# Mask, pooled scaling and value sums of batches 0 and 1 on other engines, and another order of weight chunks for the first three token tiles

## The chip, the core and the metric

The kernel runs on one core of a Trainium2 chip. A core has five engines that run their own instruction streams side by side and wait for each other by semaphores: TensorE (PE, matmuls, with its weight loads as PEld), VectorE (DVE), ScalarE (ACT), GpSimd (POOL) and SyncE (SP, which issues most DMAs). The metric is the device time of one execution in microseconds. Before the change the median of three runs is 1007.32 us.

## The reference

```python
q_d, k_d, v_d = (a.reshape(B, H, 144, 4, D).mean(axis=3) for a in (q, k, v))   # B, H, S, D = 8, 8, 576, 64
out_up = np.repeat(sm_attn(q_d, k_d, v_d), 4, axis=2)
mask = np.abs(pos[:, None] - pos[None, :]) < 4
scores = np.where(mask, scale * q @ k.T, -1e9)            # scale = 1 / 8
out_local = softmax(scores) @ v
x = (out_up + out_local).transpose(0, 2, 1, 3).reshape(4608, 512)
h = x @ w_in                                              # w_in 512 x 2048
out = (h * np.cos(h)) @ w_out                             # w_out 2048 x 512
```

Each head has two attentions: a pooled one over 144 means of four neighbours, and a local one in which a query sees only the keys within three positions. Their sum is the input of a feed-forward layer with the activation h cos h. The weights come as 64-bit floats.

## The kernel before

**Feed-forward.** The 4608 tokens are cut into 12 tiles of 384, and the 2048 hidden features into 16 chunks of 128. A step is one tile with one chunk: `gemm1` makes h (12 matmuls, since x and the weights are each split into a high and a low part), ScalarE and VectorE make h cos h and split it again (lines 748 to 757), and two steps later `gemm2` multiplies by the chunk of `w_out` into three PSUM banks (9 matmuls, line 775). The list `PASSES` (line 36) says in which order tiles and chunks are taken. Tiles 3 to 11 take all 16 chunks at one stretch. Tiles 0 to 2 take four chunks at a time in turn, tile by tile, because the weights of later chunks are not there yet. At the end of each stretch the banks are evacuated and stored; a later stretch of the same tile adds to what is in DRAM (a DMA from GpSimd, line 800).

**Weights.** Each chunk has two halves of 512 KB, one of `w_in`, one of `w_out`. `w_load` brings a half, `w_split` turns the 64-bit words into a high and a low 32-bit part: one operation on ScalarE, four on VectorE (lines 421, 423, 425, 427), then a copy and a subtraction.

**Attention.** A unit is one batch with a pair of heads; there are 32. Its steps are

- `u_qk`: loads of q and k, and the pooling of both (line 490 on VectorE, or 483 and 485 on GpSimd).
- `u_v`: loads of v, and the sums of four neighbours in two additions (lines 504 and 505, on either engine).
- `u_s`: local scores (`l_mm`, line 546) and pooled scores (`d_mm`, line 555) into two PSUM banks; the mask is added on the way out of PSUM (line 569), then maximum (574), subtraction (399), exponentials on ScalarE (594 and 597 for batches 0 and 1), sums (609), reciprocal (611 and 613), and scaling of both parts by it (615, or 621 on ScalarE for the pooled part of batches 0 and 1).
- `u_t`: transposes of the pooled weights on TensorE (line 648), evacuated by line 465 or 466; the local weights are transposed by VectorE (line 632).
- `u_pv`: products with the values, pooled (line 665) and local (677), and their sum (lines 465 and 696), which is copied into x (lines 711 and 399).

`NEARLY = 2`: batches 0 and 1 are done in a form of their own, ahead of everything else, since tile 0 is made of batch 0 alone and tile 1 of batches 0 and 1. Their units borrow the places of weight chunks that have not come yet. Three PSUM banks serve `u_s`, `u_t` and `u_pv` of batch 1 in turn, so a pair's scores wait until the pair before has given up its banks.

**What sets the order.** All operations go into a plan with an assumed duration, and a list scheduler (`Plan`) decides in which order each engine takes them; operations with `alts` may go to another engine, and it decides that too. When an assumed duration, an engine or the order of the steps changes, the order on all engines changes. While TensorE would be idle early in the program, line 892 has it multiply an identity to no purpose.

## Time and profile before

| | |
|---|---|
| median of three runs | 1007.32 us (1006.21 to 1008.86) |
| the profiled execution | 1007.4 us, of which the profile's span is 1005.6 us |
| TensorE busy | 981.2 us (98% of the span) |
| VectorE busy | 681.7 us (68%) |
| ScalarE busy | 610.2 us (61%) |
| GpSimd busy | 221.3 us (22%) |
| mean granted clock of TensorE | 0.988 |
| `gemm1` matmuls, line 739 | 2304, 338 ns each in the record, overlapping |
| `gemm2` matmuls, line 775 | 1728, 396 ns each in the record, overlapping |

A row of a group reads: line, engine, operation, output and inputs by the program's names, their shapes, count, busy us, mean ns of one, then the idle time of the engine before them and what ended it. A row of the timeline begins with the start and the length in us. A row of the windows begins with the stretch and its length, then each engine's busy time with its number of instructions, the clock of TensorE, the share of the DMA engines and GB/s. Matmuls overlap, so the length of one in the record is longer than its share of the time. Names such as wxi and wxo are weight places that a unit borrows.

### The profile page before, as it was taken

Reading aid. Unit: us, or ns where it says so; the run is one execution under the profiler, and the core shown is the slowest. Engines: PE = TensorE matmul, PEld = TensorE weight load, DVE = VectorE, ACT = ScalarE, POOL = GpSimd, SP = SyncE. Lnnn points to the kernel's source line nnn. Section 1 sums busy time; section 2 is a strip of 40 time slices with the busy share of each in tenths; the row PEclk is TensorE's granted clock in tenths of the full one; section 3 lists DMA queues with packets and bytes.
Section 4 is the critical chain, followed back from the end, with each engine's and each line's share of the span. In section 5 each row is a group of like instructions: output and inputs, shape, how many; then the busy total and the mean of one; then the engine's idle time right before and its main releaser. Section 6 shows DMA issues by size and latency. Waiting matters only on the chain.

```text
span 1005.6 us, 23855 instructions
## 1 busy us (share of the span) xinstructions
PE 981.2 (98%) x9917; PEld 847.3 (84%) x9917; DVE 681.7 (68%) x1362; ACT 610.2 (61%) x1174; POOL 221.3 (22%) x280
## 2 busy tenths in 40 slices
PE   8878999999999999999999999999999999999998
PEld 4546899899887888889888888888888888899997
DVE  7799899986587578464758957655657865433433
ACT  3457588876576656555547746654646665655554
POOL 6775325631153202000002211200001300000000
PEclk9979799999999999999999999999999999999999
DMA  7784643424355322210212312201112320100000
GB/s 224 234 270 149 215 159 64 80 36 68 67 116 132 78 65 70 68 33 28 81 49 71 129 49 58 83 26 36 62 54 73 112 65 4 37 1 1 32 1 32
DMA packets 41051, 80.70 MB, mean 80 GB/s; under 512 B 4976, under 2 KB 16240, under 8 KB 40944
## 3 DMA queue, kind: packets, MB, share of 16 engines
q1 hardware_dynamic: 37056, 72.11, 23.2%
q0 software_dynamic: 3888, 7.08, 5.0%
q8 instruction: 78, 1.28, 0.5%
q14 instruction: 29, 0.24, 0.1%
HBM read 57.93 MB, written 16.52 MB: 74 GB/s over the span
## 4 chain that ended last, share of the span: by engine, by line
PE 87%; DVE 6%; DMA 4%; issue 1%; ACT 1%; SPq 0%; ACTq 0%; DVEq 0%
PE bank L775 38%; PE bank L739 38%; PE bank L539 2%; PE bank L684 2%; PE bank L555 2%; PE bank L665 2%; PE bank L648 1%; DMA q<-qT 1%; DMA wdi<-w_in 1%; PE bank L892 1%; PE bank L677 1%; DMA vl<-vl 1%; DVE su L609 1%; DMA wxi<-qT 0%; DVE wxo L615 0%
## 5 line engine op out<-in xcount | busy, mean ns | idle before, releaser
L775 PE MATMUL bank<-wo,gh 128*128 128x512 f32 x1152 | 363.5, 396 | 0.0
L775 PEld LDWEIGHTS bank<-wo,gh 128*128 128x128 f32 x1152 | 210.0, 188 | 38.0 <-issue 3.1
L775 PE MATMUL bank<-wo,gl 128*128 128x512 f32 x576 | 227.6, 396 | 0.0
L750 ACT ACTIVATE tr<-bank,bmagic 128x384 f32<-128x384 f32 x192 | 110.9, 577 | 113.5 <-PE bank L739 109.7
L754 DVE SCALAR_TENSOR_TENSOR tr<-tr,bank 128x384 f32<-128x384 f32 x192 | 105.0, 547 | 108.0 <-ACT tr L749 107.1
L751 DVE SCALAR_TENSOR_TENSOR tr<-tr,bank 128x384 f32<-128x384 f32 x192 | 105.6, 550 | 84.2 <-ACT tr L750 83.2
L748 ACT ACTIVATE tr<-tr 128x384 f32<-128x384 f32 x192 | 100.7, 524 | 77.0 <-DVE tr L751 76.4
L756 ACT ACTIVATE gh<-tr 128x384 fp32r<-128x384 f32 x163 | 85.3, 523 | 88.3 <-DVE tr L754 86.8
L399 DVE TENSOR_TENSOR gl<-tr,gh 128x384 fp32r<-128x384 f32 x154 | 92.4, 600 | 63.5 <-ACT gh L756 60.5
L775 PEld LDWEIGHTS bank<-wo,gl 128*128 128x128 f32 x576 | 108.0, 187 | 23.5
L739 PE MATMUL bank<-x0h,wi 128*128 128x384 f32 x384 | 107.5, 340 | 0.0
L739 PE MATMUL bank<-x1h,wi 128*128 128x384 f32 x384 | 107.1, 339 | 0.0
L739 PE MATMUL bank<-x2h,wi 128*128 128x384 f32 x384 | 106.8, 338 | 0.0
L739 PE MATMUL bank<-x3h,wi 128*128 128x384 f32 x384 | 106.5, 338 | 0.0
L749 ACT ACTIVATE tr<-tr 128x384 f32<-128x384 f32 x192 | 100.8, 525 | 6.1
L399 POOL TENSOR_TENSOR gl<-tr,gh 128x384 fp32r<-128x384 f32 x38 | 43.0, 1132 | 269.6 <-DVE gh L757 175.8
L739 PEld LDWEIGHTS bank<-x0h,wi 128*128 128x128 f32 x384 | 70.5, 189 | 2.6 <-issue 0.5
L739 PEld LDWEIGHTS bank<-x1h,wi 128*128 128x128 f32 x384 | 70.3, 188 | 2.6 <-issue 0.6
L739 PEld LDWEIGHTS bank<-x2h,wi 128*128 128x128 f32 x384 | 70.2, 188 | 2.3 <-issue 0.4
L739 PEld LDWEIGHTS bank<-x3h,wi 128*128 128x128 f32 x384 | 70.2, 188 | 2.0
L739 PE MATMUL bank<-x0l,wi 128*128 128x384 f32 x192 | 64.6, 337 | 0.0
L739 PE MATMUL bank<-x3l,wi 128*128 128x384 f32 x192 | 64.6, 336 | 0.0
(199 smaller groups left out, 1452.6 us busy)
## 6 DMA issues: line engine op xcount, KB each, us to landing
vl<-vl SPq DMA_DIRECT2D x26, 384.0 KB
out<-ob SPq DMA_DIRECT2D x36, 256.0 KB
wdi<-w_in SPq DMA_DIRECT2D x16, 512.0 KB
wdo<-w_out SPq DMA_DIRECT2D x16, 512.0 KB
q<-qT SPq DMA_DIRECT2D x26, 292.0 KB
k<-kT SPq DMA_DIRECT2D x26, 292.0 KB
vd<-vdn SPq DMA_DIRECT2D x26, 288.0 KB
out<-ob POOLq DMA_DIRECT2D x27, 256.0 KB, 5.2
```

The source lines that it names most:

```text
L399: f = lambda e: lambda: e.tensor_tensor(out=out(), in0=in0(), in1=in1(), op=ALU.subtract)
L539: pe.matmul(banks[h].get()[BS * g:BS * (g + 1), c:c + BS], q.get()[hs, o:o + BS], k.get()[hs, o:o + BS], start=True, stop=True)
L555: pe.matmul(banks[h].get()[:HD, i * SD:(i + 1) * SD], qkd.get()[hs, 0, i * HD:(i + 1) * HD], qkd.get()[hs, 1, :], start=True, stop=True)
L665: pe.matmul(banks[0].get()[64 * h:64 * h + 64, 2 * SD:3 * SD], vd.get()[:, kh, 64 * h:64 * h + 64], ptd.get()[:, h, kh, :], start=(kh == 0 ...
L739: pe.matmul(ph.get()[:, :m], w[:, i, kc, :], x[:, kc, :], start=(n == 0), stop=(n == 3 * KC - 1))
L748: act.activation(tr.get(), tr.get(), AF.Sin, scale=PI)
L749: act.activation(tr.get(), tr.get(), AF.Square)
L750: pl.op("ACT", _act(m, True, 1), lambda: act.activation(tr.get(), h(), AF.Identity, bias=bmagic), r=[ph], w=[tr])
L751: pl.op("DVE", _dve(m), lambda: dve.scalar_tensor_tensor(out=tr.get(), in0=tr.get(), scalar=MAGIC, in1=h(), op0=ALU.subtract, op1=ALU.subt ...
L754: pl.op("DVE", _dve(m), lambda: dve.scalar_tensor_tensor(out=tr.get(), in0=tr.get(), scalar=0.5, in1=h(), op0=ALU.subtract, op1=ALU.mult), ...
L756: pl.op("ACT", _act(m, False), lambda: act.activation(gh.get(), tr.get(), AF.Copy), r=[tr], w=[gh], alts=[("DVE", _dve(m / 2), lambda: dve ...
L775: pe.matmul(o, (gh, gh, gl)[k].get()[:, sl], wo.get()[:, (0, 1, 0)[k]], start=(c == c0 and k == 0), stop=(c == c1 - 1 and k == 2))
```

## The change

It has four parts.

1. *Mask.* For batches 0 and 1, two matmuls of an identity with the mask (now bf16) write the mask into both PSUM banks, and the local scores are accumulated on it. VectorE then takes the maxima and subtracts them straight from PSUM, one half (192 columns) at a time, in place of an addition, a maximum over 384 columns and a subtraction over 384 columns.
2. *Pooled scaling.* For batches 0 and 1 it always goes to ScalarE, as four instructions; it was GpSimd, VectorE or ScalarE as the planner saw fit.
3. *Value sums.* For batches 0 and 1 the sums of four neighbours are not made; the pooled product takes the four rows one after another, 16 accumulated matmuls (32 instructions) in place of 4 (8 instructions).
4. *Order of chunks.* Tiles 0 to 2 take chunks 0 to 3 in turn, then chunks 4 to 7, then chunks 8 to 15 at one stretch, in place of four stretches of four.

```diff
-PASSES = [(t, c, c + NF) for c in range(0, NC, NF) for t in range(3)] + [(t, 0, NC) for t in range(3, NT)]
+PASSES = [(t, c, e) for c, e in ((0, NF), (NF, 2 * NF), (2 * NF, NC)) for t in range(3)] + [(t, 0, NC) for t in range(3, NT)]
...
-    mask = const.tile([P, NSEG + 1, BS], F32, name="mask")
+    mask = const.tile([P, NSEG + 1, BS], BF16, name="mask")
...
         dma(4 * P * 12 * D, lambda: sp.dma_start(vt.get(), vl[b, pr]), w=[vt])
+        if b < NEARLY:
+            st[(b, pr)].update(vd=vd4, vl=vt)
+            return
...
+            if b < NEARLY:
+                for h in range(2):
+                    pe.matmul(banks[h].get()[:, LQ:LQ + NSEG * BS], ident_b, mask[:, h:h + NSEG].rearrange("p s n -> p (s n)"),
+                              start=True, stop=False)
...
-                                  q.get()[hs, o:o + BS], k.get()[hs, o:o + BS], start=True, stop=True)
+                                  q.get()[hs, o:o + BS], k.get()[hs, o:o + BS], start=False, stop=(n % NSEG == NSEG - 1))
         if b < NEARLY:
-            pl.op("PE", 0.95, l_mm, r=[q, k], pw=banks, w=loc)
+            pl.op("PE", 1.3, l_mm, r=[q, k], pw=banks, w=loc)
...
+        if b < NEARLY:
+            for h in range(2):
+                mx = pl.buf(None)
+                using(banks[h], pl.op("DVE", _dve(NSEG * BS), lambda h=h: dve.tensor_reduce(
+                    out=segs(mxl, h), in_=lq(h), axis=AX.X, op=ALU.max), r=[loc[h]], pw=[mxl], w=[mx]))
+                using(banks[h], pl.op("DVE", _dve(NSEG * BS), lambda h=h: dve.tensor_tensor(
+                    out=segs(sml, h), in0=lq(h), in1=segs(mxl, h).unsqueeze(2).broadcast_to([P, NSEG, BS]), op=ALU.subtract),
+                    r=[loc[h], mx], pw=[sml]))
...
-                alts.append(("ACT", 4 * _act(SD, False, 1), scaled))
-            pl.op("POOL", _pool(size), f(pool), r=[su], w=[sm], alts=alts, shares=True)
+                pl.op("ACT", 4 * _act(SD, False, 2), scaled, r=[su], w=[sm])
+            else:
+                pl.op("POOL", _pool(size), f(pool), r=[su], w=[sm], alts=alts, shares=True)
...
+            if b < NEARLY:
+                for i in range(8):
+                    for h in range(2):
+                        pe.matmul(banks[0].get()[64 * h:64 * h + 64, 2 * SD:3 * SD], vd.get()[:, i, 64 * h:64 * h + 64],
+                                  ptd.get()[:, h, i // 4, :], start=(i == 0), stop=(i == 7))
+                return
...
-            pl.op("PE", 0.64, d_mm, r=[vd, ptd], pw=[banks[0]], w=[poo])
+            pl.op("PE", 2.1, d_mm, r=[vd, ptd], pw=[banks[0]], w=[poo])
```

The lines below the edits move down by up to 24: 546 becomes 553 for the scores, 555 becomes 562, 648 becomes 666, 665 becomes 684, 677 becomes 701, 739 becomes 763, 775 becomes 799.

Three places show how the planner's order moves. The first is TensorE where the last pair of batch 1 takes its turn (L648 and L666 are the transposes of the third pair, L546 and L553 the local scores of the last pair, L555 and L562 its pooled scores, L665 and L684 the pooled product of the third pair, L739 a step of tile 0, L775 and L799 `gemm2` of an earlier step). Before:

```order
L648 MATMUL bank<-ident,wxo_197 72x72 x8
L546 MATMUL bank<-wxo_933,wxo_923 32x32 x48
L555 MATMUL bank<-wxi_214 72x144 x4
L665 MATMUL bank<-wxi_200 64x144 x4
L739 MATMUL bank<-x0h,wi_1488 128x384
```

And now:

```order
L666 MATMUL bank<-ident,wxo_199 72x72 x4
L799 MATMUL bank<-wo_1226,gh 128x512 x2
L799 MATMUL bank<-wo_1226,gl 128x512
L666 MATMUL bank<-ident,wxo_199 72x72 x4
L538 LDWEIGHTS ident_b
L538 MATMUL bank<-mask,ident_b 128x192
L538 LDWEIGHTS ident_b
L538 MATMUL bank<-mask,ident_b 128x192
L553 MATMUL bank<-wxo_974,wxo_909 32x32 x48
L562 MATMUL bank<-wxi_205 72x144 x4
L684 MATMUL bank<-wxi_202,wxo_495 64x144 x16
```

The longer pooled product (16 matmuls in the place of 4) stands behind the next pair's scores, as before; the fourth step of tile 0 stood behind it and has moved ahead of the transposes.

The second place is VectorE at the sums of the third pair of batch 1 (L609 and L626 are its sums, L611, L613 and L628, L630 the reciprocal, L615 the pooled scaling, L632 and L650 its local transpose; L421 to L427 and L399 with a name wo are weights, L696 and L720 the addition for the second pair, L751, L754, L775 and L778 belong to steps). Before:

```order
L609 TENSOR_REDUCE su<-wxo_390 128x12
L432 CAST wi_1488<-xxh 128x512
L611 TENSOR_SCALAR su<-su 128x16
L427 SCALAR_TENSOR_TENSOR xxh<-wdo_948,xxh 128x512
L613 RECIPROCAL su<-su 128x16
L696 TENSOR_TENSOR wxi_308<-bank,wxi_276 128x3x96
L615 TENSOR_TENSOR wxo_197<-wxo_197,su 72x576
L696 TENSOR_TENSOR wxi_308<-bank,wxi_276 128x3x96
L632 STREAM_TRANSPOSE wxo_390<-wxo_390 128x384
```

And now:

```order
L626 TENSOR_REDUCE su<-wxo_399 128x12
L399 TENSOR_TENSOR wo_1506<-xxh,wo_1506 128x512
L628 TENSOR_SCALAR su<-su 128x16
L423 TENSOR_SCALAR xxh<-xxh 128x512
L630 RECIPROCAL su<-su 128x16
L425 SCALAR_TENSOR_TENSOR xxh<-wdo_1284,xxh 128x512
L778 SCALAR_TENSOR_TENSOR tr<-tr,bank 128x384
L427 SCALAR_TENSOR_TENSOR xxh<-wdo_1284,xxh 128x512
L650 STREAM_TRANSPOSE wxo_399<-wxo_399 128x384
```

The scaling has left VectorE, and more of the weights' operations stand between the pair's own.

The third place is SyncE, where the last halves of the weights are fetched (wdi and wdo are halves of `w_in` and `w_out`, out is a store of a stretch's result, ptb, q and vd belong to batch 2). Before:

```order
L797 DMA out<-ob 128x512 x3
L410 DMA wdi_2019<-w_in 128x4x256
L410 DMA wdo_2051<-w_out 128x1024
L410 DMA wdi_2063<-w_in 128x4x256
L410 DMA wdo_2095<-w_out 128x1024
L410 DMA wdi_2107<-w_in 128x4x256
L410 DMA wdo_2138<-w_out 128x1024
L410 DMA wdi_2151<-w_in 128x4x256
L797 DMA out<-ob 128x512 x3
L410 DMA wdo_2210<-w_out 128x1024
```

And now:

```order
L410 DMA wdi_2059<-w_in 128x4x256
L821 DMA out<-ob 128x512 x2
L410 DMA wdo_2110<-w_out 128x1024
L821 DMA out<-ob 128x512
L410 DMA wdi_2147<-w_in 128x4x256
L410 DMA wdo_2163<-w_out 128x1024
L410 DMA wdi_2192<-w_in 128x4x256
L410 DMA wdo_2206<-w_out 128x1024
L476 DMA q<-qT 128x584
```

All weights are now fetched ahead of the stores of tiles 1 and 2's first stretch, which stood in part before the last half.

More of the change, by code (lines that the diff above doesn't have):

```diff
@@ L567, in u_s @@
         pl.op("POOL", 0.15, lambda: pool.memset(su.get(), 1.0), w=[su])
-        for h in range(2):
-            using(banks[h], pl.op("DVE", _dve(NSEG * BS), lambda h=h: dve.tensor_tensor(
-                out=sml.get()[:, NSEG * h:NSEG * (h + 1)], in0=banks[h].get()[:, LQ:LQ + NSEG * BS].rearrange("p (s n) -> p s n", n=BS),
-                in1=mask[:, h:h + NSEG] if b < NEARLY else band, op=ALU.add), r=[loc[h]] + zeroed[:1], pw=[sml]))
         n = 2 * NSEG * BS
         bl = lambda t: t.unsqueeze(2).broadcast_to([P, 2 * NSEG, BS])
-        pl.op("DVE", _dve(n), lambda: dve.tensor_reduce(out=mxl.get(), in_=sml.get(), axis=AX.X, op=ALU.max), r=[sml], w=[mxl])
-        sub(n, sml.get, sml.get, lambda: bl(mxl.get()), r=[mxl], w=[sml])
+        segs = lambda t, h: t.get()[:, NSEG * h:NSEG * (h + 1)]
+        lq = lambda h: banks[h].get()[:, LQ:LQ + NSEG * BS].rearrange("p (s n) -> p s n", n=BS)
+        if b < NEARLY:
[8 more added lines that the diff above has]
+            for h in range(2):
+                using(banks[h], pl.op("DVE", _dve(NSEG * BS), lambda h=h: dve.tensor_tensor(
+                    out=segs(sml, h), in0=lq(h), in1=band, op=ALU.add), r=[loc[h]] + zeroed[:1], pw=[sml]))
+            pl.op("DVE", _dve(n), lambda: dve.tensor_reduce(out=mxl.get(), in_=sml.get(), axis=AX.X, op=ALU.max), r=[sml], w=[mxl])
+            sub(n, sml.get, sml.get, lambda: bl(mxl.get()), r=[mxl], w=[sml])
         mxd = sb("mxd", 2, [HD, 2, 2])
@@ L621, in scaled @@
                             act.activation(smd.get()[:, h, i], smd.get()[:, h, i], AF.Copy, scale=sud()[:, h, i:i + 1])
-                alts.append(("ACT", 4 * _act(SD, False, 1), scaled))
-            pl.op("POOL", _pool(size), f(pool), r=[su], w=[sm], alts=alts, shares=True)
+                pl.op("ACT", 4 * _act(SD, False, 2), scaled, r=[su], w=[sm])
+            else:
+                pl.op("POOL", _pool(size), f(pool), r=[su], w=[sm], alts=alts, shares=True)
         u["sml"], u["smd"] = sml, smd
@@ L662, in d_mm @@
         def d_mm():
+            if b < NEARLY:
+                for i in range(8):
+                    for h in range(2):
+                        pe.matmul(banks[0].get()[64 * h:64 * h + 64, 2 * SD:3 * SD], vd.get()[:, i, 64 * h:64 * h + 64],
+                                  ptd.get()[:, h, i // 4, :], start=(i == 0), stop=(i == 7))
+                return
             for kh in range(2):
```

## The prediction

> **What bounds the kernel now.** I read the windows first, cut where the first step of token tile 1 begins, because from there on the steps follow one another without a break.
>
> ```profile
> core 0: us, PE busy (x) PEld busy (x) DVE busy (x) ACT busy (x) POOL busy (x), PEclk, DMA share, GB/s
> 0.00:110.47 110.47, 93.06 (x2023) 60.40 (x2024) 94.33 (x185) 58.03 (x164) 69.48 (x107) 0.89 0.69 215
> 110.47:1005.60 895.13, 888.17 (x7896) 786.86 (x7894) 587.34 (x1178) 552.20 (x1010) 151.80 (x173) 1.00 0.24 64
> ```
>
> After 110.47 us TensorE is busy for 888 of 895 us at full clock. Of the 7 idle us, the waits of that stretch on TensorE itself account for 2.7; what is left lies mostly behind the last matmul:
>
> ```profile
> PE bank L684 <- DMA ptb<-sml: 1.5, 3, 0.9
> PE bank L648 <- DVE smd L615: 0.8, 1, 0.8
> PE bank L539 <- ACT ptd L465: 0.4, 1, 0.4
> ```
>
> So nothing done to VectorE, ScalarE or GpSimd can shorten the second stretch by more than 2.7 us, and only work that TensorE gains or loses there counts. The change touches batches 0 and 1 only, and their matmuls stand ahead of 110.47. What it can win is an earlier start of tile 1. Before that, TensorE has only four steps to do, and the timeline shows them as islands (first matmul of steps 0 to 3, then of step 4, which is tile 1 on chunk 0):
>
> ```profile
> 47.61 0.52 PE L739 MATMUL bank<-x0h,wi 128*128 128x384 f32 x1
> 65.34 0.88 PE L739 MATMUL bank<-x0h,wi 128*128 128x384 f32 x1
> 77.39 0.44 PE L739 MATMUL bank<-x0h,wi 128*128 128x384 f32 x1
> 90.73 0.44 PE L739 MATMUL bank<-x0h,wi 128*128 128x384 f32 x1
> 110.47 0.60 PE L739 MATMUL bank<-x1h,wi 128*128 128x384 f32 x1
> ```
>
> Step 4 needs x1, and x1 needs all four pairs of batch 1. Between the islands each pair runs through the same chain: scores on TensorE, maxima and subtraction on VectorE, exponentials on ScalarE, sums and scaling, transposes, products with the values, addition. The last pair of batch 1 ends like this:
>
> ```profile
> 100.44 1.03 PE L648 MATMUL bank<-ident,wxi 72*72 72x72 f32 x8 [1.68 <-DVE wxi L615]
> 102.25 1.23 PE L665 MATMUL bank<-wxo 72*64 72x144 f32 x8
> 103.41 2.77 PE L677 MATMUL bank<-wxi,wxo 32*64 32x24 f32 x96
> 107.93 1.44 PE L539 MATMUL bank<-k,q 64*32 64x32 f32 x96
> 109.30 1.24 PE L555 MATMUL bank<-qkd 64*72 64x144 f32 x8
> ```
>
> VectorE is busy for 94 of the first 110 us, GpSimd for 69. The first stretch is a chain through a VectorE that is nearly full and that GpSimd slows down; the rows of the next part show how much.
>
> **The change part by part.** The times are those of the profiled execution (1007.4 us, 0.1 above the median of the runs). These are the VectorE rows before 107.4 us that the change removes or replaces:
>
> ```profile
> L569 DVE TENSOR_TENSOR wxi<-bank,mask 128x192 f32<-128x192 f32 x8 | 2.4, 340 | 1.4 <-PE bank L555 1.4
> L574 DVE TENSOR_REDUCE mxl<-wxi 128x12 f32<-128x384 f32 x4 | 2.1, 538 | 0.0
> L399 DVE TENSOR_TENSOR wxi<-wxi,mxl 128x384 f32<-128x384 f32 x4 | 3.6, 890 | 0.0
> L399 DVE TENSOR_TENSOR wxo<-wxo,mxl 128x384 f32<-128x384 f32 x1 | 0.5, 543 | 0.0
> L615 DVE TENSOR_TENSOR wxo<-wxo,su 72x576 f32<-72x576 f32 x2 | 4.1, 2041 | 0.0
> L615 DVE TENSOR_TENSOR wxi<-wxi,su 72x576 f32<-72x576 f32 x3 | 3.5, 1163 | 0.0
> L615 DVE TENSOR_TENSOR smd<-smd,su 72x576 f32<-72x576 f32 x1 | 0.7, 739 | 0.0
> L504 DVE TENSOR_TENSOR wxi<-wxi 72x512 f32<-72x512 f32 x1 | 1.5, 1505 | 0.4 <-DMA wxi<-vdn 0.4
> L504 DVE TENSOR_TENSOR vd<-vd 72x512 f32<-72x512 f32 x2 | 1.6, 784 | 0.9 <-DMA vd<-vdn 0.9
> ```
>
> *Mask in PSUM.* Per pair, two mask adds (2 x 0.340), one maximum (0.538) and one subtraction (0.890 on average, 0.543 where it is undisturbed) make 2.11 us. In their place come two maxima and two subtractions read from PSUM, each 128x192. No row has these forms; the mask add, also 128x192 from PSUM, is nearest: 4 x 0.340 = 1.36. The pair's chain gets 0.75 us shorter. [...] On TensorE the pair gets two identity matmuls 128x192 in bf16; the warm-up matmul is the same with 512 columns, so 2 x 0.433 x 192/512 = 0.3 us, between nothing (hidden while the chain waits elsewhere) and 0.87 (no cheaper than the wide one).
>
> ```profile
> L892 PE MATMUL bank<-ident_b 128*128 128x512 bf16 x125 | 38.7, 433 | 1.4 <-POOL ident_b masks.py:199 1.4
> L621 ACT ACTIVATE smd<-smd,su 72x144 f32<-72x144 f32 x4 | 1.3, 404 | 3.0 <-DVE su L613 3.0
> ```
>
> On the path stand the four pairs of batch 1: 4 x (0.3 - 0.75) = -1.8 us. In batch 0 the loads arrive so late that I count nothing.
>
> *Pooled scaling on ScalarE.* Six of the eight ran on VectorE, two on ScalarE at 1.3 us for four instructions. For the second to fourth pair of batch 1 I compare 1.16, 2.04 and 0.74 with 3 x 1.3: 0.0 us on the path, between -2.2 (the slow ones were all on it) and +1.7 (they had been hidden). What is queued behind it on ScalarE are the evacuations of the transposes, which wait for it anyway. VectorE loses 8.3 us of work.
>
> *Value sums inside the products.* The pooled product grows from 8 to 32 TensorE instructions. Two rows bound its price, at full and at half clock:
>
> ```profile
> 27.64 0.71 PE L665 MATMUL bank<-wxo 72*64 72x144 f32 x8
> 52.00:56.00 4.00, 1.53 (x8) 0.49 (x5) 3.97 (x9) 1.96 (x9) 1.93 (x2) 1.00 0.86 218
> 56.00:66.00 10.00, 8.45 (x128) 5.35 (x129) 8.60 (x15) 3.90 (x12) 9.61 (x12) 0.51 0.90 258
> 100.50:110.50 10.00, 10.00 (x223) 6.84 (x223) 8.20 (x18) 4.19 (x11) 1.66 (x3) 0.50 0.50 172
> ```
>
> 24 more instructions cost 24 x 0.71/8 = 2.1 us, or 24 x 1.23/8 = 3.7 at half clock. For six of the eight pairs the order puts the product right behind the next pair's scores, while VectorE and ScalarE work on those: hidden. For the last pair of each batch nothing covers it: +2.1 twice, 4.2 us on the path (7.4 at half clock). That cover would be gone for the others if VectorE became much faster; each would then cost its 2.1.
>
> What leaves with it are the sums, 3.1 us of VectorE in the two L504 rows above, and five on GpSimd:
>
> ```profile
> L504 POOL TENSOR_TENSOR wxi<-wxi 72x512 f32<-72x512 f32 x3 | 4.7, 1577 | 7.7 <-DMA wxi<-vdn 7.7
> L505 POOL TENSOR_TENSOR wxo<-wxi 72x256 f32<-72x256 f32 x3 | 2.3, 769 | 0.2
> L483 POOL TENSOR_TENSOR wxi<-wxo 128x144 f32<-128x144 f32 x4 | 2.6, 642 | 0.0
> L485 POOL TENSOR_TENSOR wxi<-wxi,wxo 128x144 f32<-128x144 f32 x8 | 5.6, 703 | 0.6
> ```
>
> *What the planner does with the room.* It refills VectorE, at the prices of these rows:
>
> ```profile
> L490 DVE TENSOR_REDUCE wxi<-wxi 128x144 f32<-128x576 f32 x2 | 1.5, 744 | 0.1
> L421 DVE TENSOR_SCALAR xxh<-xxh 128x512 f32<-128x512 f32 x10 | 5.1, 519 | 0.0
> L423 DVE TENSOR_SCALAR xxh<-xxh 128x512 int32<-128x512 int32 x10 | 6.9, 702 | 0.0
> L425 DVE SCALAR_TENSOR_TENSOR xxh<-wdi,xxh 128x512 int32<-128x512 int32 x5 | 4.1, 825 | 0.0
> L427 DVE SCALAR_TENSOR_TENSOR xxh<-wdi,xxh 128x512 int32<-128x512 int32 x4 | 2.8, 697 | 0.0
> ```
>
> Counted in the order up to the last pair's addition, VectorE takes six more poolings of q and k (6 x 0.744 = 4.5 us) and three more half chunks of weights (3 x 2.74 = 8.2). That is 12.7 us in, against 8 x 0.75 + 8.3 + 3.1 = 17.4 out: its total hardly falls. GpSimd's does: 5 x (1.58 + 0.77) = 11.7 us of sums go, and six poolings (12 before, 6 now) at 0.64 + 2 x 0.70 = 2.05, 12.3 us. From 69 us to some 45. That is the main term: the rows above have the same operation at 0.54 and 0.89, at 0.74, 1.16 and 2.04, at 0.78 and 1.51, and the long ones are from times when GpSimd was busy. The removed operations alone carry 4 x 0.35 + 3 x 0.42 + 2 x 1.30 + 0.72 = 6.0 us of such delay. For what stays on VectorE the trace has no undisturbed copy of each row; with 24 of 69 GpSimd us gone I take 5 us earlier for the chain, between 1 and 9. And since the scaling and the sums no longer stand in VectorE's queue ahead of another pair's chain, a further 0 to 6 us (8.3 + 3.1, less the 4.5 of moved poolings and the part of the scalings that I compared with ScalarE); I take 2.5, less than half, because the planner fills the place with weights.
>
> *Chunks 8 to 15 at one stretch.* TensorE does the same matmuls. Nine evacuations and nine accumulating stores fall away, which nobody waited for: none of the three waits above names them. The weights of chunks 12 to 15 are needed eight steps earlier. In the order all 32 half chunks are split before the VectorE work of step 26 stands in its queue, chunk 15 being needed at step 31: 0 us, at most 2.7 won or a like amount lost.
>
> *Sum:* -1.8 + 0.0 + 4.2 - 5 - 2.5 = -5.1, and with the 2.7 us of later waits left as they are, step 4 begins at about 105.4 and the execution takes 1007.4 - 5.1 = 1002.3 us.
>
> **The rivals.**
>
> *The room goes into weights.* The three extra half chunks stand in VectorE's queue between the chain's steps. If they cost the chain what the relief brings, step 4 comes between 108 and 113 and the time is about 1007. For it: VectorE was busy 94 of 110 us, so any filler delays something. Against: the planner puts them where the chain waits for ScalarE. 0.23.
>
> *VectorE was the whole bound.* Then the chain follows the work that must be done, which falls by the 17.4 us less the 4.5 of moved poolings: 12.9 us, 994.5. Against: the wait of 1.68 us above is for one single operation, so latency counts too. 0.13.
>
> *Slower: half clock under the longer products.* Place: the last pair of each batch, between its transposes and the addition. The windows show 0.51 behind a stretch in which TensorE was busy for 1.53 of 4 us, and 0.50 from 100.5 us on, behind a wait of only 1.68. If both products run at half clock they cost 7.4 instead of 4.2, and the local product of batch 0, which takes 2.77 at half clock, costs 1.4 more than at full: -1.8 + 7.4 + 1.4 = +7.0 against what relief and queue bring. With my 7.5 for those it comes out even; below 4 together the change is slower by over 3 us; with 2 it is 5.0 slower, 1012.4. [...] 0.09.
>
> *Slower: late weights.* Chunks 8 to 15 are taken one per step. If their splits ran behind, TensorE would wait at steps 24 to 31, perhaps 1 us at each: 1007.4 - 5.1 + 8 = 1010. Against: the order. 0.05.
>
> **How the numbers follow.** The forecast has 0.50, and its own range is 999 to 1005. The range of 8 in 10 adds the VectorE-bound case and the case without gain: 994.5 to 1008.5. A difference of 0.3% is 3.0 us, about what a measurement of this kernel can tell from no change. Faster by more than that: 0.43 of the forecast's 0.50, 0.13 and 0.07 of the first rival make 0.63. Within: 0.07 of the forecast, 0.14 of the first rival, 0.02 of the slower ones, 0.23. Slower: 0.12 of the slower ones and 0.02 of the first rival, 0.14.
>
> **What would show it.** In the profile after: the first matmul of x1h at 103 to 108 us; GpSimd below 50 us ahead of it; TensorE busy all but 7 us of what follows, with some 895 us from there to the end; maxima and subtractions from PSUM near 0.34 us; the pooled product at 2.8 us, unless the clock column stands at 0.5 there. I am wrong in the main term if VectorE's rows stay as long although GpSimd is less busy, or if x1h begins at 110 although they got shorter; wrong in the rest if new waits of TensorE appear between steps 24 and 48.

## The result and the profile after

The changed kernel takes 1011.7 us (median of 18 runs, 1007.7 to 1021.6), the kernel before 1005.2 (18 runs, 1001.5 to 1012.0). The ratio is 1.0058, with a 95% interval of 1.0040 to 1.0076: slower by 5.8 us (4.0 to 7.6; the two medians themselves are 6.5 apart), where 5.1 less were forecast. In what follows 0.1% is 1.0 us.

The profiled execution of the changed kernel is its longest (1021.6 us, mean clock of TensorE 0.979; its median clock is 0.992), so about 10 of its microseconds are not typical. The windows of the changed kernel, cut at step 4, and its batch 0 and batch 1 parts:

```profile
core 0: us, PE busy (x) PEld busy (x) DVE busy (x) ACT busy (x) POOL busy (x), PEclk, DMA share, GB/s
0.00:122.58 122.58, 111.64 (x2212) 79.35 (x2212) 86.82 (x200) 64.15 (x187) 44.09 (x74) 0.83 0.65 209
122.58:1019.80 897.22, 888.87 (x7897) 786.80 (x7895) 585.38 (x1164) 546.22 (x1001) 142.65 (x163) 1.00 0.21 59
...
0.00:63.95 63.95, 58.01 (x1139) 38.82 (x1140) 33.68 (x84) 22.75 (x78) 17.69 (x47) 0.76 0.66 202
63.95:122.58 58.63, 53.63 (x1073) 40.53 (x1073) 53.15 (x117) 41.40 (x110) 26.40 (x27) 0.91 0.64 216
```

The same two parts of the kernel before:

```profile
0.00:47.60 47.60, 41.27 (x1041) 24.05 (x1042) 35.57 (x75) 19.44 (x67) 32.44 (x66) 0.96 0.77 233
47.60:110.47 62.87, 51.78 (x984) 36.35 (x983) 58.76 (x111) 38.59 (x98) 37.04 (x42) 0.84 0.63 201
```

Of 14.2 us more span, 12.1 lie ahead of step 4 and 2.1 behind it. Batch 1's part became 4.2 us shorter, as a relief would make it, but its clock is 0.91 against 0.84, so this alone does not show the relief. Batch 0's part became 16.3 us longer, at a clock of 0.76 against 0.96, and there VectorE is idle half the time while TensorE is nearly full. How much of the 16.3 is the clock, a run below shows. The timeline of TensorE in batch 0 of the changed kernel (start, length) shows it taking pair after pair almost without a gap:

```profile
23.45 1.47 PE L701 MATMUL bank<-sml,vl 32*64 32x24 f32 x87 [1.60 <-issue]
24.86 0.61 PE L916 MATMUL bank<-ident_b 128*128 128x512 bf16 x2
25.39 4.02 PE L684 MATMUL bank<-ptd,vd 72*64 72x144 f32 x32
29.34 1.03 PE L916 MATMUL bank<-ident_b 128*128 128x512 bf16 x2
30.17 0.69 PE L666 MATMUL bank<-ident,wxi 72*72 72x72 f32 x4
30.65 1.06 PE L916 MATMUL bank<-ident_b 128*128 128x512 bf16 x2
31.86 0.67 PE L666 MATMUL bank<-ident,wxi 72*72 72x72 f32 x4
32.31 1.06 PE L916 MATMUL bank<-ident_b 128*128 128x512 bf16 x2
33.31 2.77 PE L701 MATMUL bank<-wxi,wxo 32*64 32x24 f32 x96
36.01 1.03 PE L916 MATMUL bank<-ident_b 128*128 128x512 bf16 x2
36.97 4.11 PE L684 MATMUL bank<-wxo,wxi 72*64 72x144 f32 x32
...
59.16 2.18 PE L684 MATMUL bank<-wxo,wxi 72*64 72x144 f32 x32
```

The window of that stretch, with TensorE busy for 30.46 of 30.61 us and the clock (third number from the end) at 0.50:

```profile
25.39:56.00 30.61, 30.46 (x427) 22.19 (x427) 12.63 (x29) 8.91 (x24) 5.09 (x8) 0.50 0.63 194
```

The pooled product (L684) takes 4.0 to 4.1 us here, at half clock; at full clock (1.00 from 56.3 to 60.0 us) it takes 2.18, where I had 2.8. L916 are the idle multiplications. The new VectorE forms cost what was forecast (0.347 and 0.343 for 0.34), and the rows whose length the prediction put down to GpSimd are shorter (line 423 from 702 to 503 ns):

```profile
L582 DVE TENSOR_REDUCE mxl<-bank 128x6 f32<-128x192 f32 x16 | 5.0, 347 | 4.1 <-PE bank L562 4.1
L584 DVE TENSOR_TENSOR wxi<-bank,mxl 128x192 f32<-128x192 f32 x8 | 2.5, 343 | 0.0
L423 DVE TENSOR_SCALAR xxh<-xxh 128x512 int32<-128x512 int32 x13 | 6.5, 503 | 0.0
```

Behind step 4 TensorE has these waits in the changed kernel, in place of the three shown of the kernel before:

```profile
PE bank L763 <- DVE tr L778: 2.4, 3, 1.1
PE bank L708 <- DMA ptb<-sml: 1.0, 2, 0.5
PE bank L666 <- DVE smd L632: 0.5, 1, 0.5
```

So the rows came out as priced, and the end did not: the first matmul of x1h stands at 122.6 although they got shorter (behind 110 even without the 10 us that are not typical), which is the prediction's own sign that its main term was wrong.

### The profile page after: what moved, and what is told of

Its sections match the earlier page's. It is cut to its first block, busy times and chain, and to the rows that moved or that the text cites. A ratio compares the mean times of both kernels' runs of the same rounds, so it can differ in the third digit from the quotient of the medians.

```text
span 1019.8 us, 24171 instructions
## 1 busy us (share of the span) xinstructions
PE 1000.5 (98%) x10106; PEld 866.1 (85%) x10106; DVE 672.2 (66%) x1363; ACT 610.4 (60%) x1187; POOL 186.7 (18%) x236
## 4 chain that ended last, share of the span: by engine, by line
PE 76%; DVE 4%; DMA 2%; ACT 1%; issue 1%; SPq 1%; ACTq 0%; DVEq 0%
PE bank L799 34%; PE bank L763 34%; PE bank L546 2%; PE bank L708 2%; PE bank L562 1%; PE bank L689 1%; PE bank L666 1%; DMA ptb<-sml 1%; DMA k<-kT 1%; SPq L657 1%; DVE xxh L423 1%; DVE tr L778 1%; DVE xxh L425 0%; DVE xxh L427 0%; DVE tr L775 0%
## 5 line engine op out<-in xcount | busy, mean ns | idle before, releaser
L799 PE MATMUL bank<-wo,gh 128*128 128x512 f32 x1152 | 364.0, 397 | 0.0
L799 PEld LDWEIGHTS bank<-wo,gh 128*128 128x128 f32 x1152 | 209.7, 188 | 38.6 <-issue 3.5
L799 PE MATMUL bank<-wo,gl 128*128 128x512 f32 x576 | 227.7, 396 | 0.0
L778 DVE SCALAR_TENSOR_TENSOR tr<-tr,bank 128x384 f32<-128x384 f32 x192 | 105.0, 547 | 110.8 <-ACT tr L773 109.9
L775 DVE SCALAR_TENSOR_TENSOR tr<-tr,bank 128x384 f32<-128x384 f32 x192 | 105.6, 550 | 83.2 <-ACT tr L774 81.7
L780 ACT ACTIVATE gh<-tr 128x384 fp32r<-128x384 f32 x155 | 81.2, 524 | 88.1 <-DVE tr L778 86.6
L399 DVE TENSOR_TENSOR gl<-tr,gh 128x384 fp32r<-128x384 f32 x156 | 93.2, 598 | 61.6 <-ACT gh L780 58.9
L799 PEld LDWEIGHTS bank<-wo,gl 128*128 128x128 f32 x576 | 108.0, 188 | 23.5
L763 PE MATMUL bank<-x0h,wi 128*128 128x384 f32 x384 | 108.2, 342 | 3.3 <-DVE tr L778 2.7
L399 POOL TENSOR_TENSOR gl<-tr,gh 128x384 fp32r<-128x384 f32 x36 | 42.6, 1184 | 250.9 <-DVE gh L781 168.7
L763 PE MATMUL bank<-x2l,wi 128*128 128x384 f32 x192 | 64.5, 336 | 0.0
```

The costliest lines, as they stand in the source:

```text
L399: f = lambda e: lambda: e.tensor_tensor(out=out(), in0=in0(), in1=in1(), op=ALU.subtract)
L763: pe.matmul(ph.get()[:, :m], w[:, i, kc, :], x[:, kc, :], start=(n == 0), stop=(n == 3 * KC - 1))
L775: pl.op("DVE", _dve(m), lambda: dve.scalar_tensor_tensor(out=tr.get(), in0=tr.get(), scalar=MAGIC, in1=h(), op0=ALU.subtract, op1=ALU.subt ...
L778: pl.op("DVE", _dve(m), lambda: dve.scalar_tensor_tensor(out=tr.get(), in0=tr.get(), scalar=0.5, in1=h(), op0=ALU.subtract, op1=ALU.mult), ...
L780: pl.op("ACT", _act(m, False), lambda: act.activation(gh.get(), tr.get(), AF.Copy), r=[tr], w=[gh], alts=[("DVE", _dve(m / 2), lambda: dve ...
L799: pe.matmul(o, (gh, gh, gl)[k].get()[:, sl], wo.get()[:, (0, 1, 0)[k]], start=(c == c0 and k == 0), stop=(c == c1 - 1 and k == 2))
```

## The experiments

Theory 1: the long products stand in series on TensorE in batch 0, in all four pairs. Theory 2: the stretch of chunks 8 to 15 costs the time. Theory 3: the mask or the scaling does. Later a fourth: the order that the planner makes anew. For each run the table gives the ratio to the kernel before, timed on the same chip, with its interval; step 0, step 4 and what follows to the end of the span are from one profiled execution each, and ahead of step 4 these executions differ in clock (0.78 to 0.95).

| run | median us | ratio (95%) | step 0 | step 4 | rest |
|---|---|---|---|---|---|
| before | 1005.2 | 1 | 47.6 | 110.5 | 895.1 |
| changed | 1011.7 | 1.0058 (1.0040, 1.0076) | 64.0 | 122.6 | 897.2 |
| e1 sums apart | 1006.5 | 1.0018 (0.9997, 1.0039) | 53.9 | 114.8 | 895.1 |
| e2 products only | 1019.4 | 1.0125 (1.0097, 1.0153) | 51.4 | 114.2 | 903.3 |
| e3 old order | 1018.5 | 1.0113 (1.0078, 1.0149) | 60.2 | 116.0 | 902.5 |
| e4 new order only | 1008.5 | 1.0026 (1.0005, 1.0047) | 50.0 | 111.6 | 895.1 |
| all products short | 1005.8 | 1.0022 (1.0002, 1.0042) | 49.4 | 108.2 | 897.6 |
| batch 0 short | 1005.0 | 0.9994 (0.9970, 1.0018) | 46.2 | 106.4 | 896.4 |
| last pairs short | 1008.4 | 1.0036 (1.0017, 1.0055) | 53.9 | 110.0 | 898.2 |
| e5 no idle work | 1014.2 | 1.0100 (1.0082, 1.0119) | 62.3 | 121.5 | 895.6 |
| before, products of 56 | 1022.9 | 1.0175 (1.0139, 1.0211) | 64.7 | 130.0 | 895.4 |
| e7 mask and scaling | 1014.7 | 1.0098 (1.0065, 1.0130) | 47.1 | 109.7 | 902.7 |
| splits held | 1015.1 | 1.0093 (1.0067, 1.0120) | 52.4 | 111.1 | 899.3 |
| batch 1 only, held | 1006.2 | 1.0020 (0.9998, 1.0042) | 48.0 | 106.0 | 896.1 |
| before, products of 32 | 1011.5 | 1.0055 (1.0025, 1.0086) | 53.8 | 116.9 | 895.8 |
| before without sums | 1000.3 | 0.9924 (0.9894, 0.9953) | 44.6 | 101.7 | 893.8 |
| both, order of before | 1011.7 | 1.0043 (1.0013, 1.0072) | 57.7 | 121.2 | 893.5 |
| e6 batch 1 only | 1008.0 | 1.0012 (0.9984, 1.0040) | 48.6 | 112.8 | 896.1 |
| without sums, replanned | 1012.9 | 1.0082 (1.0052, 1.0111) | 46.5 | 108.5 | 900.1 |
| changed, no sums, replanned | 1004.9 | 0.9976 (0.9948, 1.0003) | 50.8 | 109.7 | 895.5 |

**Parts alone and parts undone.** First the changed kernel with the sums made apart:

> The changed kernel with the value sums made apart again (8 instructions per pooled product instead of 32), all else as changed. Theory 1, the long products: in batch 0 TensorE takes pair after pair in series, so 24 more instructions per pair are 2.1 us at full clock on the path each, and a TensorE that is filled with narrow matmuls loses the clock. Then this kernel has step 0 at 46 to 50 us instead of 64, no stretch of 30 us at half clock, and takes 1002 to 1006 us, level with the kernel before or up to 3 us faster. Theory 2, the stretch of chunks 8 to 15: stays at 1010 to 1012, with the waits of gemm1 for VectorE's tr between 150 and 200 us. Theory 3, mask or ScalarE scaling: stays at 1009 or more with step 0 later than 55 us.

```diff
-        if b < NEARLY:
-            st[(b, pr)].update(vd=vd4, vl=vt)
-            return
...
-            pl.op("PE", 2.1, d_mm, r=[vd, ptd], pw=[banks[0]], w=[poo])
+            pl.op("PE", 0.64, d_mm, r=[vd, ptd], pw=[banks[0]], w=[poo])
```

Then the kernel before with that part of the change alone (e2), the changed kernel with the old stretches (e3), and the kernel before with the new ones alone (e4):

> The kernel before with the value sums inside the pooled products and nothing else. Theory 1: batch 0 later by 4 x 2.1 = 8 us at full clock and up to 15 at half clock, a part given back in batch 1; 1009 to 1015 us. Theory 2 or 3: GpSimd and VectorE are relieved at no price, 1000 to 1005 us.

```diff
+        if b < NEARLY:
+            st[(b, pr)].update(vd=vd4, vl=vt)
+            return
...
-            pl.op("PE", 0.64, d_mm, r=[vd, ptd], pw=[banks[0]], w=[poo])
+            pl.op("PE", 2.1, d_mm, r=[vd, ptd], pw=[banks[0]], w=[poo])
```

> The changed kernel with the four stretches of four chunks as before. Theory 1: 1009 to 1012 us, step 0 at 52 to 64 us as in the changed kernel, half clock in batch 0 in the profile. Theory 2: 1004 to 1007 us, the waits of gemm1 for tr (4.8 us in the changed kernel) gone and step 0 still late. The waits may go without the time following, which would give theory 2 a part of 2 to 3 us.

```diff
-PASSES = [(t, c, e) for c, e in ((0, NF), (NF, 2 * NF), (2 * NF, NC)) for t in range(3)] + ...
+PASSES = [(t, c, c + NF) for c in range(0, NC, NF) for t in range(3)] + ...
```

> The kernel before with chunks 8 to 15 at one stretch and nothing else. Theory 1: within 2 us of the kernel before, step 0 at 47 to 49, step 4 at 109 to 112. Theory 2: 1009 to 1012, with TensorE waiting in gemm1 between steps 12 and 48.

```diff
-PASSES = [(t, c, c + NF) for c in range(0, NC, NF) for t in range(3)] + ...
+PASSES = [(t, c, e) for c, e in ((0, NF), (NF, 2 * NF), (2 * NF, NC)) for t in range(3)] + ...
```

Without the products the changed kernel is about level with the one before (e1), and the products alone cost 12.5 us (e2): theory 1, but 12.5 is more than the changed kernel's 5.8. Theory 2 falls: with the old stretches the changed kernel is not faster but 5.5 us slower (e3), though the new stretches alone cost 2.6 (e4). The last column says where: e2 and e3 have 902 to 903 us behind step 4, where the kernel before, with the same stretches in another order, has 895. From 300 to 345 us, where tile 3 begins, the windows of e3 and of the changed kernel are

```profile
300.00:345.00 45.00, 39.90 (x544) 32.77 (x540) 33.33 (x72) 30.34 (x56) 14.20 (x17) 1.00 0.52 112
```

```profile
300.00:345.00 45.00, 45.00 (x621) 38.95 (x621) 37.07 (x82) 31.65 (x57) 14.78 (x20) 1.00 0.39 104
```

TensorE idles for 5.1 us in e3, for nothing in the changed kernel, and for 2.7 in the kernel before. Tile 3 waits there for batch 2. In e2 it idles for 4.2 us, and the clock of the window is 0.92, so this execution loses more there than the idle time; in e3 the clock of the window stayed at 1.00.

**Mask and scaling alone**, with the old stretches; the edit stands against the changed kernel:

> The kernel before with the mask in PSUM and the pooled scaling on ScalarE, without the value sums in the products and with the old order of chunks. The prediction's terms: 1.8 us faster from the mask and 0 (-2.2 to +1.7) from the scaling, 1000 to 1004 us. If the chain of batch 1 did not wait for these operations: within 1 us of the kernel before.

```diff
-PASSES = [(t, c, e) for c, e in ((0, NF), (NF, 2 * NF), (2 * NF, NC)) for t in range(3)] + ...
+PASSES = [(t, c, c + NF) for c in range(0, NC, NF) for t in range(3)] + ...
...
-        if b < NEARLY:
-            st[(b, pr)].update(vd=vd4, vl=vt)
-            return
...
-            pl.op("PE", 2.1, d_mm, r=[vd, ptd], pw=[banks[0]], w=[poo])
+            pl.op("PE", 0.64, d_mm, r=[vd, ptd], pw=[banks[0]], w=[poo])
```

9.8 us slower, with step 4 at 109.7: none of it is ahead of step 4, all of it in the 902.7 us behind. ScalarE's copies of batch 2 into x (start, length) show how:

```profile
273.88 0.53 ACT L726 ACTIVATE x3h<-vd 128x384 fp32r<-128x384 f32 x1 [1.28 <-DVE vd L711]
274.31 0.35 ACT L726 ACTIVATE x0h<-vd 128x192 fp32r<-128x192 f32 x1
287.86 0.53 ACT L726 ACTIVATE x3h<-vd 128x384 fp32r<-128x384 f32 x1 [0.19 <-DVE vd L711]
...
317.24 0.52 ACT L726 ACTIVATE x3h<-vd 128x384 fp32r<-128x384 f32 x1 [4.60 <-DVE vd L711]
```

The last third of a batch 2 pair goes to tile 4, which takes tile 0's place (x0h). With the old stretches tile 0 is read up to 264 us, in e7 and in the kernel before alike. In e7 the plan puts the two copies of each pair side by side, so all four pairs are squeezed into 274 to 317. In the kernel before the first pair's two copies stood apart, x3h early and x0h as soon as the place was free:

```profile
233.00 0.51 ACT L711 ACTIVATE x3h<-vd 128x384 fp32r<-128x384 f32 x1
263.85 0.25 DVE L712 CAST x0h<-vd 128x192 fp32r<-128x192 f32 x1
```

There TensorE waited 2.7 us. In e1, which is e7 with the new stretches, the first copy into x3h is made at 222.5, tile 0 is read up to 235, and TensorE waited 0.6. The new stretch is worth 8.0 us there (e7 to e1).

**How long the products are, in the changed kernel's own order.** In these three the order of all engines is the changed kernel's.

> The changed kernel in its own order on every engine, but each pooled product of batches 0 and 1 issues only 8 of its 32 instructions (rows 0 and 7), so three quarters of the value sums are left out. It measures what the products' length costs, without any other order. Theory 1, long products in series in both batches: 24 x 0.09 = 2.1 us less for each of 8 pairs, 17 us of TensorE, most of it on the path in batch 0, and less half clock: step 0 at 48 to 54 us, 1000 to 1004 us. The prediction's view, only the last pair of each batch counts: 4 us less than the changed kernel, 1006 to 1008. Theory 3, the new order of the other engines costs it: 1010 or more.

```diff
-                for i in range(8):
+                for i in ((0, 7) if True else range(8)):
```

> As the run with all products short, but only those of batch 0 (four pairs); batch 1 has its full 32 instructions. Left out: three quarters of batch 0's value sums. Theory 1: nearly all of the gain of the run with all short, 1001 to 1006 us, since batch 0 has nothing to hide a product behind. The prediction's view: 2.1 us less than the changed kernel, 1009.

```diff
+                for i in ((0, 7) if b == 0 else range(8)):
```

> As the run with all products short, but only those of the last pair of each batch; the other six have their full 32 instructions. Left out: three quarters of these two pairs' value sums. The prediction's view, in which the other six are hidden: as fast as the run with all short, 4 us less than the changed kernel or more. Theory 1: about a quarter of the gain, 2 to 3 us less than the changed kernel, with step 0 still after 55 us.

```diff
+                for i in ((0, 7) if pr == NPAIR - 1 else range(8)):
```

Against the changed kernel, short products in batch 0 win 6.4 us, in the last pair of each batch 2.2, in both batches 3.6. Batch 0 carries most of it; that all products together win less than batch 0's alone lies within the intervals, and in part in the clock (a median of 0.988 with all short, 0.992 in the changed kernel). Inside one kernel the runs of this record lose 6.9 us per 0.01 of mean clock, fitted over all of them; at one clock of 0.990, an estimate by this figure, all products short win about 8 us, batch 0's about 6 and the last pairs' about 3. So the length is a large part of the loss. It is not all that went wrong: with all products short the kernel is still 2.2 us slower than before, where the prediction without its 4.2 for the length would have it 9.3 faster.

**Idle multiplications.**

> The changed kernel without the minimum of two idle multiplications ahead of each TensorE step of batch 0 (those that fill planned idle time stay), 83 instructions of TensorE fewer. Theory 1 in the form that TensorE's own series bounds batch 0: some 20 of them stand between 25 and 56 us at about 0.5 us each at half clock, so step 0 comes 5 to 12 us earlier, 1003 to 1008 us. If they are what holds the clock, it is halved earlier and longer, step 0 stays after 60 and the time at 1011 or more. If loads or VectorE bound batch 0: no change.

```diff
-           fgap=0.4, f0=0.8, fend=300.0, warm=2)
+           fgap=0.4, f0=0.8, fend=300.0, warm=0)
```

Shorter series, slower kernel: all five runs have a mean clock of 0.973 to 0.977, and from 20 to 60 us TensorE is at 0.54. The second half of the expectation held.

```profile
20.00:60.00 40.00, 37.42 (x737) 32.44 (x727) 18.15 (x44) 15.06 (x50) 9.47 (x16) 0.54 0.69 212
```

**Weights held back.** The rival in which the room goes into weights:

> The changed kernel with the splits of chunks 4 to 15 held back in the planner until the last addition of batch 1: 8 half chunks are split ahead of it on VectorE, as in the kernel before, instead of 11. Rival, the room goes into weights: 3 x 2.4 = up to 7 us earlier step 4, part of it taken back by splits that are late between steps 4 and 24; 1004 to 1009 us. Theory 1, the price is in batch 0's products and what follows waits for TensorE and banks: within 2 us of the changed kernel, 1010 to 1013.

The second run has the same, and products in batch 1 alone (the edit of e6 below):

> The changed kernel with sums inside the products for batch 1 only (batch 0 has them apart, 8 instructions) and the splits of chunks 4 to 15 held back. What the runs so far point to: step 0 as in the run with batch 0 short or the run with sums apart, 46 to 54 us, and step 4 at 102 to 106 instead of 107 to 110: 998 to 1003 us. If holding the splits only moves the wait to steps 4 to 24: 1004 to 1008.

```diff
-        pl.op("ACT", _act(n, False), lambda: act.activation(v.get(), ..., AF.Abs), r=[wd_b], w=[v], shares=True)
+        o = pl.op("ACT", _act(n, False), lambda: act.activation(v.get(), ..., AF.Abs), r=[wd_b], w=[v], shares=True)
+        if c >= 4:
+            o.sdeps += ends
...
+            if (b, pr) == (1, NPAIR - 1):
+                ends.append(o)
```

With 8 half chunks ahead of batch 1's end instead of 11 the kernel is not faster (1.0093 against 1.0058). At that end VectorE has little to do and TensorE, at half clock, is the one that is late:

```profile
100.00:110.00 10.00, 9.68 (x204) 7.87 (x208) 2.79 (x9) 3.05 (x8) 0.17 (x1) 0.51 1.06 377
```

So the fillers are not what costs the time. Whether they cost the chain something at full clock stays open, since this end ran at 0.51.

This run also answers for the 30 us at half clock. Its batch 0 has as many instructions on every engine as the changed kernel's, TensorE's in the same order, and its profiled execution took them at full clock:

```profile
0.00:52.36 52.36, 45.45 (x1139) 29.78 (x1140) 33.60 (x84) 22.82 (x78) 17.68 (x47) 1.00 0.81 246
```

Step 0 begins at 52.4 here and at 64.0 in the changed kernel's profile. Of the 16.3 us by which batch 0 became longer, 11.6 are thus the clock of one execution, and 4.8 are left against the kernel before, which had 0.96 there.

The version with products in batch 1 alone is level with the kernel before, with the splits held or not:

> The changed kernel with sums inside the products for batch 1 alone, nothing held back. If batch 0 alone pays for the length: as the run with batch 0 short, 1003 to 1006 us, step 0 before 50. If batch 1 pays as well: 1007 to 1010.

```diff
-        if b < NEARLY:
+        if b == 1:
             st[(b, pr)].update(vd=vd4, vl=vt)
...
-            pl.op("PE", 2.1, d_mm, r=[vd, ptd], pw=[banks[0]], w=[poo])
+            pl.op("PE", 2.1 if b == 1 else 0.64, d_mm, r=[vd, ptd], pw=[banks[0]], w=[poo])
```

**Price and relief, one at a time, in the order of before.** These keep the order of every engine as it was before the change. The first issued 56 instructions per product, not the 32 that its text says.

> The kernel before in its own order on VectorE, ScalarE and GpSimd, with its value sums, and with each pooled product of batches 0 and 1 issued as 32 instructions instead of 8 (the 8 are done four times, the last counts), at one place of TensorE's order. The price of the length alone, with no relief. If it is what the runs with short products say, 3 to 6 us: 1007 to 1011. If length costs only with the changed order: within 2 us of the kernel before. The prediction's term was 4.2.

> The kernel before in its own order, sums made, each pooled product of batches 0 and 1 issued as 32 instructions (the pass over the 8 four times). The run with 56 was 17.5 us slower. If every instruction of all eight pairs stands in series, half of that: 8 to 9 us, 1012 to 1014. If only the last pair of each batch counts, as the prediction had it: 4 us, 1008 to 1009.

```diff
+            for j in range(3 if b < NEARLY else 0):
+                for kh in range(2):
+                    for h in range(2):
+                        pe.matmul(banks[0].get()[...], vd.get()[...], ptd.get()[...], start=(kh == 0), stop=(kh == 1))
```

> The kernel before in its own order without the value sums of batches 0 and 1: the products read row 0 of each four, so three quarters of the sums are left out; five sums on GpSimd (11.7 us) and three on VectorE (3 us) are gone, and nothing takes their place. The prediction's main term: GpSimd's relief 5 us (1 to 9) came from these sums and from six poolings, so about half of it and a part of the queue's 2.5: 3 to 5 us, 1000 to 1002. If the sums were never on the path: within 1 us of the kernel before.

```diff
+        if b < NEARLY:
+            pl.op("POOL", 2.2, lambda: None, w=[vd, vd4], alts=[("DVE", 1.1, lambda: None)], shares=True)
+            st[(b, pr)].update(vd=vd4, vl=vt)
+            return
...
-                    pe.matmul(..., vd.get()[:, kh, 64 * h:64 * h + 64],
+                    pe.matmul(..., vd.get()[:, 4 * kh if b < NEARLY else kh, 64 * h:64 * h + 64],
```

> The kernel before in its own order on all engines, value sums inside products of 32 instructions. The sum of the two runs above: 8 less the relief, 1008 to 1013. With the planner's own order the same edit took 1019; if the difference is the order, this one has TensorE wait less than 3 us between 300 and 345 us, as the kernel before.

```diff
+        if b < NEARLY:
+            pl.op("POOL", 2.2, lambda: None, w=[vd, vd4], alts=[("DVE", 1.1, lambda: None)], shares=True)
+            st[(b, pr)].update(vd=vd4, vl=vt)
+            return
...
+                for i in range(8):
```

24 instructions more per product cost 5.5 us, 48 more cost 17.5. The sums taken away win 7.6. Both together should then win 2.1, and they lose 4.3; the gap of 6.4 is a little more than the three intervals leave (about 5). A part of it is the clock: the medians are 0.987 for the kernel before, 0.990 without sums, 0.9935 with products of 32 and 0.990 with both. Set to one clock of 0.990 by the 6.9 us per 0.01 (an estimate), the length costs 9.2 us, the sums win 4.6 and both together lose 7.6, so that 3.0 of the gap are left. The windows ahead of step 4, of the kernel without sums, with products of 32, and with both:

```profile
0.00:101.72 101.72, 88.82 (x2024) 58.45 (x2024) 81.57 (x177) 57.32 (x163) 56.20 (x97) 0.95 0.74 233
```

```profile
0.00:116.91 116.91, 101.74 (x2216) 71.15 (x2216) 89.23 (x182) 57.88 (x163) 68.98 (x107) 0.94 0.65 203
```

```profile
0.00:121.21 121.21, 109.61 (x2215) 77.55 (x2215) 80.80 (x176) 57.86 (x163) 57.19 (x97) 0.87 0.63 196
```

With long products TensorE is busy for 102 to 110 us there, whether GpSimd has 57 or 69, and idles for 12 to 15; it has as many matmuls in both, and the 8 us between them go with the clock (0.94 and 0.87). VectorE's 8 us less from the second to the third make its idle time longer, from 27.7 to 40.4 us. (The three executions are 3 us below, 3 above and 5 above the medians of their kernels.)

**The planner's order.** The same work as without sums, planned anew:

> The kernel before without the value sums of batches 0 and 1 (products of 8 instructions read rows 0 and 7; three quarters of the sums left out), planned anew with the sums gone. Same work as the run without sums in the order of before, which took 1000. If the relief survives: 998 to 1002. If the planner's new order gives it away (more half chunks ahead of batch 1's end, batch 2's pairs later with the old stretches): 1004 to 1010, with waits of TensorE between 300 and 345 us of 4 us or more.

> The changed kernel with the same left out and its products priced at their short length, planned anew: mask, scaling and the stretch of chunks 8 to 15 as changed. If the long price in the plan held the order back: 998 to 1002. If mask, scaling or stretch cost it: 1004 to 1007, as the run with all products short.

In the first the sums are left out as in the run above, but with no place kept for them, and the products read rows 0 and 7. The second's edit, against the changed kernel:

```diff
-                for i in range(8):
+                for i in (0, 7):
...
-            pl.op("PE", 2.1, d_mm, r=[vd, ptd], pw=[banks[0]], w=[poo])
+            pl.op("PE", 0.64, d_mm, r=[vd, ptd], pw=[banks[0]], w=[poo])
```

The first is 15.8 us slower than the same work in the old order (1.0082 against 0.9924). Its windows ahead of and behind step 4, and at tile 3:

```profile
0.00:108.48 108.48, 94.78 (x2018) 63.04 (x2019) 90.08 (x186) 56.88 (x161) 54.48 (x91) 0.87 0.74 233
108.48:1008.60 900.12, 892.48 (x7904) 789.64 (x7902) 594.87 (x1187) 549.73 (x1006) 134.82 (x155) 1.00 0.23 62
...
300.00:320.00 20.00, 17.25 (x221) 13.84 (x219) 13.70 (x32) 10.21 (x19) 4.07 (x6) 0.85 0.52 122
```

In the two profiled executions 6.8 us are ahead of step 4 and 6.3 behind it. Ahead of it the clock is 0.87 against 0.95, TensorE is busy 6.0 us longer for as many matmuls, and VectorE for 90 us instead of 82. In the medians the clock is 0.981 against 0.990, which by the 6.9 us per 0.01 is some 6 of the 15.8 us (an estimate). The second, with mask, scaling and the new stretches, is 2.4 us faster than the kernel before, within its interval: so these three, in this plan, do not cost the ten microseconds. It leaves out three quarters of the sums; no run with the whole computation beat the kernel before.

## Why the prediction was wrong, point by point

- **What bounds the kernel.** TensorE behind step 4: right for the changed kernel (895 forecast, 897.2 measured). But I asked only what could shorten that stretch. Runs that are planned anew with the old stretches lengthen it by 7 to 8 us (e2, e3, e7).
- **Mask and scaling.** The durations were right (0.347 and 0.343 us; 0.403 for one scaling instruction). Their -1.8 and 0.0 on the path were not seen apart: e7's step 4 is 0.8 earlier, in single executions.
- **Length of the products: +4.2.** In the order of before it measures 5.5 (2.5 to 8.6), at a higher clock than the kernel before; at one clock 9.2, an estimate. So it was near as measured, by luck, and wrong in place. "For six of the eight pairs ... hidden" fails: short products in batch 0 alone win 6.4 us, in the last pair of each batch 2.2.
- **Relief: -5 and -2.5.** In the order of before the sums alone give -7.6 (4.6 at one clock, an estimate). The relief is real. But beside the long products it does not show: both together are +4.3, at one clock 7.6 against 9.2 for the length alone.
- **Chunks 8 to 15: 0.** Alone +2.6 (0.5 to 4.7), beside the other parts -5.5 (e3 to changed). I had the early weights, and not that tile 0's place comes free some 30 us earlier for batch 2. The forecast's 2.7 won at tile 3 came true, and 2.4 us of new waits for line 778 between steps 4 and 48 took it.
- **The sum.** This is the step that failed. I added -7.5 and +4.2 as if both lay on one path, which for sums and products together makes -3.3. In an unchanged order the two together measure +4.3. By the estimate at one clock the length, which batch 0 does not hide, was put at half its price, and about 3 us are left that do not add up. That fits a reading in which one part shortens VectorE's and GpSimd's chain, the other lengthens TensorE's, and the later of the two ends the batch; no run shows this by itself. The second fault is that moved work counted as a list of VectorE microseconds (12.7 in, 17.4 out), while the new order by itself moves the time by 8 (e2 against both in the order of before) to 16 us, more than any term. In both comparisons the median clock is 0.981 against 0.990, which by the 6.9 us per 0.01 is some 6 us of it (an estimate). Taken from the changed kernel's 5.8, the 4.3 of the products leave 1.5, within the intervals, for all else; that is a remainder across two orders, not a measurement.
- **Rivals.** Weights in the room: holding them back wins nothing. VectorE the whole bound: refuted, its work ahead of step 4 fell from 94 to 87 us and the time rose. Half clock under the longer products: its 1012.4 is near the 1011.7, and the profiled execution shows its 0.50 for 30 us. That explains why this execution is 10 us above the median. It does not explain the median, so the nearness is luck: the changed kernel's median clock is 0.992 and that of the 123 runs of before taken beside the experiments 0.988, so at the median it loses no more to the clock.

What stays open: what in a plan lowers the clock ahead of step 4, and the price of mask and scaling by themselves in an unchanged order. Neither was tried.

## What to carry to other kernels

Where a planner orders the work, an edit is two edits: run it once in the old order, with the operation's place kept, and once planned anew. Gains and costs on different engines are not added unseen: ask which engine ends last with all of them in place. Where the runs of one kernel follow the clock, put the mean clock beside each median before taking differences. A step that frees a buffer early for a later batch belongs in the sum, even if nobody waits for it now.

## What the runs showed of the hardware

- Being busy did not by itself bring the clock back: TensorE stayed at 0.50 for 30.6 us in which it was busy for 30.46, with narrow matmuls for the most part. Narrow matmuls did not by themselves lose it either, which theory 1 assumes in the expectation of e1: the same ones in the same order ran at 1.00 in the run with the weights held back.
- With the minimum of two idle 128x512 multiplications ahead of each step gone, the mean clock was low in all five runs (0.973 to 0.977, against a median of 0.992 in the changed kernel).
- TensorE stops for "issue" in the middle of a group of matmuls, with no semaphore that the profile shows: 1.60 us in the changed kernel ahead of 23.45 us, 2.86 in the kernel with products of 56 ahead of 34.75 us (x6, then x41, of one product). The DMA share was 0.75 during the first and 0.84 from 30 to 40 us around the second. Half clock followed both: in the changed kernel the clock is 1.00 up to 25.4 us and 0.54 from there to 27.0, in the other it is 0.63 from 30 to 40 us. Where the changed kernel stops for 1.60 us, the run with the weights held back stops for 0.23 at the same matmul and keeps its clock; a stop of 1.06 us at 26 us in the kernel with products of 56 left the clock at 1.00 too (20 to 30 us). Why it stops was not tried. The kernel with products of 56, then the run with the weights held back:

```profile
31.19 0.70 PE L666 MATMUL bank<-wxo 72*64 72x144 f32 x6
34.75 5.30 PE L666 MATMUL bank<-wxo 72*64 72x144 f32 x41 [2.86 <-issue]
...
22.05 1.47 PE L703 MATMUL bank<-sml,vl 32*64 32x24 f32 x87 [0.23 <-issue]
23.99 2.18 PE L686 MATMUL bank<-ptd,vd 72*64 72x144 f32 x32
```

- Runs of one program differ with the clock they are granted: the changed kernel took 1009.8 us at a mean of 0.995 and 1021.6 at 0.979. Over all kernels of this record the slope inside one kernel is 6.9 us per 0.01.
